# A bias build with both ends of a tile on one engine, and score steps with two pieces instead of four

## The chip, the cores and the metric

The kernel runs on one core of a Trainium2 chip. Its engines are TensorE (PE), which multiplies matrices into the accumulators in PSUM; VectorE (DVE) and ScalarE (ACT), which both read PSUM and SBUF; GpSimd (POOL), which works on SBUF alone; and SyncE (SP), whose queue issues the DMAs here. Each engine takes its instructions in the order in which they were written for it and waits at semaphores for the others. The metric is the device time of one execution, in microseconds (us).

## What is computed

Three layers follow each other: attention with a learned bias by position, and two MLPs that each token passes through. Only attention matters here. There are 4 batches, 8 heads, 576 positions and 64 values a head.

```
scores = scale * np.matmul(q, k.transpose(0, 1, 3, 2))
pos = np.arange(S)
rel = (pos[:, None] - pos[None, :]).astype(np.float32)
psi_rel = np.log1p(np.abs(rel))
psi_i = np.log1p(np.maximum(pos[:, None].astype(np.float32), 1.0))
x = (psi_rel / psi_i)[..., None]
h = np.maximum(x @ w1 + b1, 0.0)
bias = h @ w2
scores = scores + bias.transpose(2, 0, 1)[None, :, :, :]
```

A softmax over the keys and the product with `v` follow. The bias is a sum of 32 hidden relus for every query, distance and head.

## The kernel before

**The bias build** is a generator, `bias_phase`, of 36 steps of 16 queries each (`k` counts them) and one more for the last store. A step is `produce(k)` and `store(k - 1)`. `produce` makes four relu tiles `y`, one for each group of four queries, over N distances, where N falls from 576 to 304 and rises again to 576. The first `na` of the four (one or two) are made by ACT (line 64), the others by DVE (line 66); the list `NA` says how many, and `relu_split` fills it with a greedy plan that adds up estimated costs for both engines. PE then sums the 32 hidden values of each tile (line 71), each group into its own 32 partitions of a PSUM tile `bt`, of which there are two. `store` makes one tile `e` out of `bt`: ACT writes the distances forwards (line 80, 576 - 16k elements), DVE the same distances backwards (line 81, 16k + 15 elements), and SP stores `e` to DRAM (line 83, 295.5 KB). Four tiles `e` go round, and ten relu tiles (`YBUF`). Two small constants `cb`, which the stores add, come out of four matmuls of one column (line 50) that stand behind the first step's sums.

`during(k)` hangs other work into the steps: the loads of the first unit's q, k and v (`load_raw`, `load_v`) and of the identity ahead of the first step, four splits of raw q and k into a high and a low part in steps 6 to 9 (ACT line 170, POOL line 174), two loads of weights in steps 3 and 4, two of the second unit's q and k, and the loads of the finished bias tiles (line 151), which wait for the stores of the rows that they read. 28 steps run alone (`ALONE`), the others four at a time in the first steps of attention: steps 28 to 31 stand ahead of the first scores on PE, 32 to 35 ahead of the second.

**Attention** runs over 16 units, one for each batch and pair of heads. A unit has five steps. In steps 0 to 3 two score tiles are made, for 128 queries of the first head and 128 of the second, each with 64 contraction rows of PE's array so that the two run side by side. The fifth step makes one tile, `t == 8`, for the last 64 queries of both heads, with all 128 rows: q is block diagonal there. q and k are each a high and a low part, so a step has three passes (high-high, low-high, high-low), which add up in PSUM (`scores`, line 213). k is stored with 64 columns at the front for the second head's last keys and 64 at the end for the first head's. So tile 8, which needs both heads' last keys in the same columns, takes them as two pieces of 64 columns, each with zeros in the other head's rows:

```
LAST_TILE = ((0, 64, 288),), ((0, 352, 224), (224, 576, 64), (224, 0, 64))
```

DVE then adds the bias and takes the minimum (`reduce_min`, line 228), ACT takes the exponential, POOL divides by the sum, PE transposes (lines 256 to 265) and multiplies by v (lines 303, 306). Score tiles have two buffers, `sc`, so the scores of a step wait for the reduces of the step before. DVE also carries the conversion of weights for the MLPs in the gaps (lines 493 to 495 and 491).

Of the kernel before, what the change touches and what calls it, by code (L numbers as in the profile page):

```python
# [7 lines left out]
F32 = mybir.dt.float32  # L8
# [19 lines left out]
def bias_phase(tc, pools, par, c_log, bsc, during):  # L28

    nc = tc.nc  # L30
    V, A, G, T = nc.vector, nc.scalar, nc.gpsimd, nc.tensor
    yp, ep, pp, spare = pools
    pr = yp.tile([128, PAR], F32, name="pr", bufs=1)
    nc.sync.dma_start(pr, par)
    lg = yp.tile([128, S], F32, name="lg", bufs=1)
    nc.sync.dma_start(lg, dram_ap(c_log, 0, [[0, 128], [1, S]]))
    during(-1)
    w1c, b1c, wb, ps = pr[:, 0:1], pr[:, 1:2], pr[:, 2:34], pr[:, 34:PAR]
    scl = yp.tile([128, S // 4], F32, name="scl", bufs=1)
    V.tensor_scalar(scl, ps, w1c, None, ALU.mult)  # L40
    nb1 = yp.tile([128, 1], F32, name="nb1", bufs=1)
    V.tensor_scalar(nb1, b1c, -1.0, None, ALU.mult)
    cb = yp.tile([128, 2], F32, name="cb", bufs=1)
    live = {}

    def constants():
        pc = spare.tile([128, 2, 512], F32, name="sc")
        V.memset(cb, 0.0)
        for gr in range(4):
            T.matmul(pc[32 * gr:32 * gr + 32, 0, 0:1], wb, b1c, start=True, stop=True)  # L50
        V.tensor_scalar(cb[64:128, 0:1], pc[64:128, 0, 0:1], 8.0, None, ALU.mult)
        V.tensor_scalar(cb[32:64, 1:2], pc[32:64, 0, 0:1], 8.0, None, ALU.mult)
        V.tensor_scalar(cb[64:128, 1:2], pc[64:128, 0, 0:1], 8.0, None, ALU.mult)

    def produce(k):
        N = max(S - 16 * k, 16 * k + 16)
        na = NA[k]
        bt = pp.tile([128, 2, 512], F32, name="bt")
        ys = []
        for gr in range(4):  # L60
            n = 4 * k + gr
            y = yp.tile([128, S], F32, name="y")
            if gr < na:
                A.activation(y[:, 0:N], lg[:, 0:N], AF.Relu, bias=b1c, scale=scl[:, n:n + 1])
            else:
                V.tensor_scalar(y[:, 0:N], lg[:, 0:N], scl[:, n:n + 1], nb1, ALU.mult, ALU.max)  # L66
            ys.append(y)
        parts = [(0, 0, N)] if N <= 512 else [(0, 0, 512), (1, 512, N - 512)]
        for hf, o, w in parts:
            for gr in range(4):  # L70
                T.matmul(bt[32 * gr:32 * gr + 32, hf, 0:w], wb, ys[gr][:, o:o + w], start=True, stop=True)  # L71
        live[k] = bt, na

    def store(k):
        bt, na = live.pop(k)
        ct = cb[:, 2 - na:3 - na]
        flat = bt.rearrange("p a b -> p (a b)")
        nf, nr = S - 16 * k, 16 * k + 15
        e = ep.tile([128, S + 16], F32, name="e")
        A.activation(e[:, nr:nr + nf], flat[:, 0:nf], AF.Identity, bias=ct, scale=8.0)  # L80
        V.tensor_scalar(e[:, 0:nr], flat[:, nr:0:-1], 8.0, ct, ALU.mult, ALU.add)
        r0 = 128 * (k % 8) * BW
        nc.sync.dma_start(dram_ap(bsc[k // 8], r0 + S - nr, [[BW, 128], [1, nf + nr]]), e[:, 0:nf + nr])

    K = S // 16
    for k in range(K + 1):
        if k < K:
            produce(k)
        if k == 0:
            constants()  # L90
        if k >= 1:
            store(k - 1)
        during(k)
        yield


A0 = 3500.0


def relu_split():  # L100

    a, v = A0, 0.0
    r = []
    for k in range(S // 16):
# [1 line left out]
        n = max(nf, nr + 1)  # L106
        cost = []
        for na in (1, 2):
            cost.append((a + na * (160 + 1.04 * n) + 50 + 1.04 * nf, v + (4 - na) * (180 + 0.54 * n) + 120 + 1.1 * nr, na))
        a, v, na = min(cost, key=lambda x: max(x[:2]))  # L110
        r.append(na)
    return r


NA = relu_split()
PAR = 34 + S // 4
NU = NP * NB
STEP_TILES = ((0, 1), (2, 3), (4, 5), (6, 7), (8,))
# [2 lines left out]
GROUP = (0, 0, 1, 1, 2)  # L121
GW = (256, 320)
QK = S + 64
LAST_TILE = ((0, 64, 288),), ((0, 352, 224), (224, 576, 64), (224, 0, 64))
ON_ACT = (1, 3, 5, 7)


def attention_phase(tc, qT, kT, vP, ident_d, par, c_log, bsc, xs, after_bias, load_weight, filler, tail):
# [5 lines left out]
    with ExitStack() as st, ExitStack() as early:  # L134
# [39 lines left out]
            G.tensor_sub(l, raws.pop((u, i)), h.bitcast(F32))  # L174

        def during(k):
            if k < 0:
                alloc(0)
                for i in range(2):
                    load_raw(0, i)  # L180
# [6 lines left out]
            if k in LW:  # L187
                load_weight()
            for t in range(9):
                if k == min(8 * (t // 2) + 10, S // 16):  # L190
                    load_bias(0, t)

        psr = lambda st, n, k: st.enter_context(tc.tile_pool(name=n, bufs=k, space=PSUM, side="right"))
# [9 lines left out]
        def scores(u, s):  # L203
# [4 lines left out]
            for i, (q, k) in enumerate(((qh, kh), (ql, kh), (qh, kl))):  # L208
                for hf in range(2):
                    for a, t in enumerate(tiles):  # L210
                        r = slice(0, 128) if t == 8 else slice(64 * a, 64 * a + 64)
                        for x, y, n in LAST_TILE[hf] if t == 8 else ((0, 288 * hf + 64 * (1 - a), 288),):
                            T.matmul(sc[u, t][:, hf, x:x + n], q[r, 128 * s:128 * s + 128], k[r, y:y + n],  # L213
                                     start=(i == 0 and x == 0), stop=(i == 2 and x + n == S // 2 and (t < 8 or y < 512)))

        def reduce_min(u, t):
            s = sc.pop((u, t))
# [174 lines left out]
EBUF = 4  # L392
LR = (16, 19)
LW = (3, 4)
YBUF = 10
ALONE = 28
PER = 4
TR = 0
# [429 lines left out]
def _layout(inputs):  # L828
# [10 lines left out]
    qt = np.concatenate([qt[..., :512], tail], axis=3)  # L839
    kw = np.zeros((NB, NP, 128, S + 64), np.float32)  # L840
    kw[:, :, :, 64:576] = kt[..., :512]
    kw[:, :, :64, 576:] = kt[:, :, :64, 512:]
    kw[:, :, 64:, :64] = kt[:, :, 64:, 512:]
    kt = kw
    vp = np.zeros((NB, NP, 128, 5, 2, D), np.float32)
# [33 lines left out]
```

## Time and profile before

| | us |
|---|---|
| time before, median of 3 runs | 1211.99 (1210.79 to 1212.88) |
| profiled execution, its own time | 1211.65 |
| span of the profiled execution | 1209.5 |
| PE busy in the span | 1183.5 |
| DVE busy | 703.9 |
| ACT busy | 623.4 |
| POOL busy | 508.6 |

The span goes from the first to the last instruction of the profiled execution. Busy time of PE counts overlapping matmuls once, up to ends that are modelled; it is no measure of how well PE is used. The bias build fills the first 64 us of the span, the rest of the bias steps and the first score steps the next 20, and attention goes on to about 340 us; the MLPs take the rest. In a row of a timeline or of grouped instructions, what stands in brackets or behind the bar is the idle time of the engine just ahead, and who ended it.

### The profile page before, as it was taken

Reading aid. Unit: us, or ns where it says so; the run is one execution under the profiler, and the core shown is the slowest. Engines: PE = TensorE matmul, PEld = TensorE weight load, DVE = VectorE, ACT = ScalarE, POOL = GpSimd, SP = SyncE. Lnnn points to the kernel's source line nnn. Section 1 sums busy time; section 2 is a strip of 40 time slices with the busy share of each in tenths; the row PEclk is TensorE's granted clock in tenths of the full one; section 3 lists DMA queues with packets and bytes.
Section 4 is the critical chain, followed back from the end, with each engine's and each line's share of the span. In section 5 each row is a group of like instructions: output and inputs, shape, how many; then the busy total and the mean of one; then the engine's idle time right before and its main releaser. Section 6 shows DMA issues by size and latency. Waiting matters only on the chain.

```text
span 1209.5 us, 19450 instructions
## 1 busy us (share of the span) xinstructions
PE 1183.5 (98%) x7280; PEld 1031.9 (85%) x7280; DVE 703.9 (58%) x1237; ACT 623.4 (52%) x1241; POOL 508.6 (42%) x488
## 2 busy tenths in 40 slices
PE   7989999999989999999999999999999999999998
PEld 2257777777769999999999999999999999999997
DVE  6889888888739898898988668872000010010100
ACT  5978778778647766767666556332211111111111
POOL 1037676776535555565555335452211212112111
PEclk9989999999999999999999999999999999999999
DMA  5753636364112323333443322530101001010000
GB/s 164 263 177 116 192 107 207 102 200 121 62 56 79 121 93 122 110 104 122 132 147 109 110 79 91 159 100 17 37 1 40 14 18 36 1 40 14 20 8 27
DMA packets 73261, 112.35 MB, mean 93 GB/s; under 512 B 8528, under 2 KB 51792, under 8 KB 73168
## 3 DMA queue, kind: packets, MB, share of 16 engines
q1 hardware_dynamic: 73168, 111.12, 29.1%
q8 instruction: 58, 0.95, 0.3%
q14 instruction: 35, 0.29, 0.1%
HBM read 81.32 MB, written 29.77 MB: 92 GB/s over the span
## 4 chain that ended last, share of the span: by engine, by line
PE 94%; DVE 2%; ACT 1%; DMA 1%; issue 1%; POOL 0%; SPq 0%; ACTq 0%; POOLq 0%; DVEq 0%
PE up L570 41%; PE acc L647 16%; PE acc L655 12%; PE sc L213 7%; PE pv L306 6%; PE pt L256 6%; PE bt L71 4%; PE pv L303 1%; PE pf L260 1%; DMA lg<-in_c_log 0%; DVE y L66 0%; ACT z L589 0%; PE pf L264 0%; DVE n L228 0%; DMA wraw<-in_wv 0%
## 5 line engine op out<-in xcount | busy, mean ns | idle before, releaser
L570 PE MATMUL up<-xt,w 128*128 128x384 f32 x2880 | 520.5, 335 | 0.5 <-DVE t L615 0.5
L570 PEld LDWEIGHTS up<-xt,w 128*128 128x128 f32 x2880 | 503.8, 188 | 8.0 <-issue 1.2
L625 POOL TENSOR_TENSOR gl<-t,gh 128x384 fp32r<-128x384 f32 x168 | 176.0, 1059 | 470.7 <-ACT gh L624 332.1
L617 DVE TENSOR_TENSOR t<-up,t 128x384 f32<-128x384 f32 x72 | 40.1, 556 | 309.4 <-ACT t L596 309.4
L596 ACT ACTIVATE t<-up 128x384 f32<-128x384 f32 x72 | 35.4, 492 | 332.6 <-PE up L570 332.6
L647 PE MATMUL acc<-gh,w 128*128 128x384 f32 x768 | 195.8, 335 | 2.9 <-ACT z L589 2.9
L246 POOL TENSOR_SCALAR n<-n,rec 128x576 f32<-128x576 f32 x144 | 117.6, 831 | 89.6 <-DVE rec L241 80.0
L647 PEld LDWEIGHTS acc<-gh,w 128*128 128x128 f32 x768 | 138.1, 188 | 4.7 <-ACT z L589 3.8
L655 PE MATMUL acc<-w,gh 128*128 128x512 f32 x432 | 134.3, 392 | 0.0
L647 PE MATMUL acc<-gl,w 128*128 128x384 f32 x384 | 128.4, 334 | 0.0
L228 DVE CUSTOM_DVE_ANT_0 n<-sc,bias 128x576 f32<-128x576 f32 x144 | 103.7, 753 | 41.2 <-PE sc L213 39.1
L235 ACT ACTIVATE n<-n,mn 128x576 f32<-128x576 f32 x144 | 111.5, 784 | 3.5 <-DVE mn L228 3.1
L556 POOL TENSOR_TENSOR xt<-xm,xt 128x384 fp32r<-128x384 f32 x72 | 73.7, 1039 | 62.3 <-ACT xt L555 62.2
L509 POOL TENSOR_TENSOR w<-wu,w 128x512 fp32r<-128x512 f32 x68 | 96.5, 1421 | 7.6 <-ACT w L511 7.6
L655 PEld LDWEIGHTS acc<-w,gh 128*128 128x128 f32 x432 | 80.1, 188 | 13.5
L624 ACT CAST gh<-t 128x384 fp32r<-128x384 f32 x168 | 84.8, 511 | 8.5 <-PE acc L647 3.6
L655 PE MATMUL acc<-w,gl 128*128 128x512 f32 x216 | 85.4, 395 | 0.0
L610 ACT ACTIVATE z<-z,c 128x768 f32<-128x768 f32 x48 | 45.2, 941 | 77.4 <-DVE up L609 77.4
L256 PE MATMUL pt<-ident,n 128*128 128x128 f32 x576 | 81.6, 282 | 1.8 <-DVE at L286 1.8
L611 DVE TENSOR_TENSOR t<-up,t 128x768 f32<-128x768 f32 x48 | 45.9, 957 | 62.8 <-ACT t L589 62.8
L306 PE MATMUL pv<-at,vs 128*64 128x320 f32 (+1 forms) x512 | 80.2, 425 | 0.0
L256 PEld LDWEIGHTS pt<-ident,n 128*128 128x128 f32 x576 | 62.2, 141 | 13.7 <-issue 8.3
(70 smaller groups left out, 1574.6 us busy)
## 6 DMA issues: line engine op xcount, KB each, us to landing
wraw<-in_wo SPq DMA_DIRECT2D x28, 512.0 KB, 3.6
bsc<-e SPq DMA_DIRECT2D x36, 295.5 KB, 2.8
xm<-xs SPq DMA_DIRECT2D x48, 192.0 KB, 3.3
x2s<-o SPq DMA_DIRECT2D x48, 192.0 KB, 3.7
wraw<-in_wi SPq DMA_DIRECT2D x16, 512.0 KB, 4.3
wraw<-in_wg SPq DMA_DIRECT2D x12, 512.0 KB, 3.6
wraw<-in_wv SPq DMA_DIRECT2D x12, 512.0 KB, 3.6
raw<-in_qT SPq DMA_DIRECT2D x16, 320.0 KB, 3.5
```

Source lines behind the costliest of these rows:

```text
L213: T.matmul(sc[u, t][:, hf, x:x + n], q[r, 128 * s:128 * s + 128], k[r, y:y + n], start=(i == 0 and x == 0), stop=(i == 2 and x + n == S // ...
L228: V.tensor_tensor_reduce(n.rearrange("p (a b) -> p a b", a=2), s[:, :, 0:288], bias[t].rearrange("p (a b) -> p a b", a=2), -0.125, 3.0e38, ...
L235: A.activation(n, n, AF.Exp, bias=m, scale=-1.0, accum_out=nsum[u, t // 4][:, t % 4:t % 4 + 1])
L246: G.tensor_scalar(n, n, nrec[u, t // 4][:, t % 4:t % 4 + 1], 1.0, ALU.mult, ALU.mult)
L256: T.transpose(pt[:, i], n[:, o:o + 128], ident)
L306: T.matmul(p[0][64 * a:64 * a + 64, 0:N], v[:, c - 1, a], main[:, c - 1, a * N:a * N + N], start=False, stop=(c == 4))
L509: self.nc.gpsimd.tensor_sub(w[:, 1], u, w[:, 0].bitcast(F32))
L570: T.matmul(p[:, 0:TB], w[:, a, 128 * kt:128 * kt + 128], x[:, c], start=(kt == 0 and i == 0), stop=(kt == 3 and i == 2))
L624: A.copy(h, x[:, j])
L625: G.tensor_sub(l, x[:, j], h.bitcast(F32))
L647: T.matmul(ac[blk][d][:, 0:TB], w[:, a, 128 * d:128 * d + 128], c, start=(begin and j == 0 and i == 0), stop=(end and j == NPR - 1 and i = ...
L655: T.matmul(ac[blk][d], g[:, c], w[:, a], start=(begin and i == 0), stop=(end and i == 2))
```

## The change

- The second head's last keys are stored at the end of k as well as at the front. Tile 8 then has both heads' last keys in its last 64 columns, and each pass has two pieces of 288 columns instead of four.
- `produce` makes the relus alone; the sums have a function of their own, `sums`. A step is now `produce(k)`, `store(k - 2)`, `sums(k)`, and there are 38 of them.
- `store` writes both ends of a tile `e` on one engine, ACT or DVE. The plan, `relu_split`, picks the engine together with the number of relus on ACT, with other estimated costs.
- `constants()` runs ahead of the first step, the first loads of q, k, v and the identity behind step 1, and `YBUF` is 12.

```diff
@@ bias_phase
     nc.sync.dma_start(lg, dram_ap(c_log, 0, [[0, 128], [1, S]]))
-    during(-1)
...
     def produce(k):
         N = max(S - 16 * k, 16 * k + 16)
-        na = NA[k]
-        bt = pp.tile([128, 2, 512], F32, name="bt")
+        na = SPLIT[k][0]
...
+        made[k] = ys
+
+    def sums(k):
+        N = max(S - 16 * k, 16 * k + 16)
+        ys = made.pop(k)
+        bt = pp.tile([128, 2, 512], F32, name="bt")
         parts = [(0, 0, N)] if N <= 512 else [(0, 0, 512), (1, 512, N - 512)]
         for hf, o, w in parts:
             for gr in range(4):
                 T.matmul(bt[32 * gr:32 * gr + 32, hf, 0:w], wb, ys[gr][:, o:o + w], start=True, stop=True)
-        live[k] = bt, na
+        live[k] = bt, SPLIT[k][0]
...
         e = ep.tile([128, S + 16], F32, name="e")
-        A.activation(e[:, nr:nr + nf], flat[:, 0:nf], AF.Identity, bias=ct, scale=8.0)
-        V.tensor_scalar(e[:, 0:nr], flat[:, nr:0:-1], 8.0, ct, ALU.mult, ALU.add)
+        for o, i in ((e[:, nr:nr + nf], flat[:, 0:nf]), (e[:, 0:nr], flat[:, nr:0:-1])):
+            if SPLIT[k][1]:
+                A.activation(o, i, AF.Identity, bias=ct, scale=8.0)
+            else:
+                V.tensor_scalar(o, i, 8.0, ct, ALU.mult, ALU.add)
...
-    for k in range(K + 1):
+    constants()
+    for k in range(K + 2):
         if k < K:
             produce(k)
-        if k == 0:
-            constants()
-        if k >= 1:
-            store(k - 1)
+        if k >= 2:
+            store(k - 2)
+        if k < K:
+            sums(k)
         during(k)
@@ relu_split
-A0 = 3500.0
+A0 = 2000.0
...
-            cost.append((a + na * (160 + 1.04 * n) + 50 + 1.04 * nf, v + (4 - na) * (180 + 0.54 * n) + 120 + 1.1 * nr, na))
+            for out in (0, 1):
+                ca, cv = na * (225 + 1.04 * n), (4 - na) * (225 + 0.54 * n)
+                if out:
+                    ca += 350 + 1.04 * (nf + nr)
+                else:
+                    cv += 280 + 1.05 * (nf + nr)
+                cost.append((a + ca, v + cv, na, out))
@@ during
-            if k < 0:
+            if k == 1:
                 alloc(0)
...
-                if k == min(8 * (t // 2) + 10, S // 16):
+                if k == min(8 * (t // 2) + 10, S // 16 + 1):
                     load_bias(0, t)
@@ scores
-                        for x, y, n in LAST_TILE[hf] if t == 8 else ((0, 288 * hf + 64 * (1 - a), 288),):
-                            T.matmul(sc[u, t][:, hf, x:x + n], q[r, 128 * s:128 * s + 128], k[r, y:y + n],
-                                     start=(i == 0 and x == 0), stop=(i == 2 and x + n == S // 2 and (t < 8 or y < 512)))
+                        o = 288 * hf + (0 if a else 64)
+                        T.matmul(sc[u, t][:, hf, 0:288], q[r, 128 * s:128 * s + 128], k[r, o:o + 288], start=(i == 0), stop=(i == 2))
@@ constants and layout
-YBUF = 10
+YBUF = 12
...
-    kw[:, :, :64, 576:] = kt[:, :, :64, 512:]
+    kw[:, :, :, 576:] = kt[..., 512:]
```

DVE at the start of the build, before (`scl` and `nb_141` are per-query scales and the negative bias of the relus, `cb` the constants):

```order
L40 TENSOR_SCALAR scl<-pr 128x144
L42 TENSOR_SCALAR nb_141<-pr 128x1
L66 TENSOR_SCALAR y<-lg,scl,nb_141 128x576 x3
L48 MEMSET cb 128x2
L51 TENSOR_SCALAR cb<-sc 64x1
L52 TENSOR_SCALAR cb<-sc 32x1
L53 TENSOR_SCALAR cb<-sc 64x1
L66 TENSOR_SCALAR y<-lg,scl,nb_141 128x560 x3
L81 TENSOR_SCALAR e<-bt,cb 128x15
L66 TENSOR_SCALAR y<-lg,scl,nb_141 128x544 x3
L81 TENSOR_SCALAR e<-bt,cb 128x31
```

The same place on DVE after:

```order
L47 MEMSET cb 128x2
L50 TENSOR_SCALAR cb<-sc 64x1
L51 TENSOR_SCALAR cb<-sc 32x1
L52 TENSOR_SCALAR cb<-sc 64x1
L64 TENSOR_SCALAR y<-lg,scl,nb_130 128x576 x3
L64 TENSOR_SCALAR y<-lg,scl,nb_130 128x560 x2
L64 TENSOR_SCALAR y<-lg,scl,nb_130 128x544 x3
L88 TENSOR_SCALAR e<-bt,cb 128x576
L88 TENSOR_SCALAR e<-bt,cb 128x15
L64 TENSOR_SCALAR y<-lg,scl,nb_130 128x528 x3
```

The constants moved ahead of the first relus, and the first tile `e` is whole on DVE, behind the relus of step 2 instead of step 1.

PE in the fifth step of the first unit (`kh`, `kl`, `qh`, `ql` are the high and low parts), before:

```order
L213 MATMUL sc<-kh,qh 128x288
L213 MATMUL sc<-kh,qh 128x224
L213 MATMUL sc<-kh,qh 128x64 x2
L213 MATMUL sc<-kh,ql 128x288
L213 MATMUL sc<-kh,ql 128x224
L213 MATMUL sc<-kh,ql 128x64 x2
L213 MATMUL sc<-kl,qh 128x288
L213 MATMUL sc<-kl,qh 128x224
L213 MATMUL sc<-kl,qh 128x64 x2
L256 MATMUL pt<-ident,n 128x128 x8
```

And after:

```order
L227 MATMUL sc<-kh,qh 128x288 x2
L227 MATMUL sc<-kh,ql 128x288 x2
L227 MATMUL sc<-kl,qh 128x288 x2
L269 MATMUL pt<-ident,n 128x128 x8
L273 MATMUL pf<-ident,n 128x128
```

Twelve matmuls became six; this is so in each of the 16 units, and nothing else moved on PE in attention.

SP's queue at the start, after:

```order
L35 DMA pr<-in_par 128x178
L36 DMA lg<-in_c_log 128x576
L172 DMA raw_180<-in_qT 128x640
L172 DMA raw_182<-in_kT 128x640
L178 DMA vs<-in_vP 128x640
L196 DMA ident<-in_ident 128x128
```

Before, the same six loads stand there in the same order; the move in the program moved nothing in this queue.

## Rows read from the trace of the kernel before

**Rows 1.** The page's head: span and instructions of the profiled execution.

```profile
span 1209.5 us, 19450 instructions
```

**Rows 2.** Busy us (instructions) of PE, PEld, DVE, ACT, POOL; PEclk, DMA share, GB/s.

```profile
6.40:63.50 57.10, 52.96 (x292) 17.08 (x294) 49.66 (x114) 46.97 (x83) 3.10 (x2) 1.00 0.64 223
82.00:84.00 2.00, 2.00 (x11) 2.00 (x11) 1.97 (x2) 0.59 (x2) 2.00 (x3) 0.50 1.01 315
100.00:120.00 20.00, 20.00 (x171) 14.08 (x169) 17.46 (x42) 15.84 (x41) 15.01 (x16) 1.00 0.45 132
```

**Rows 3.** Grouped instructions from 6.4 to 63.5 us: busy, mean ns, idle before.

```profile
L66 DVE TENSOR_SCALAR y<-lg,scl,nb 128x416 f32<-128x416 f32 (+17 forms) x79 | 37.9, 529 | 3.5 <-DMA lg<-in_c_log 3.4
L64 ACT ACTIVATE y<-lg,pr,scl 128x384 f32<-128x384 f32 (+17 forms) x49 | 33.8, 727 | 4.3 <-DMA lg<-in_c_log 4.3
...
L80 ACT ACTIVATE e<-bt,cb 128x576 f32<-128x576 f32 (+30 forms) x31 | 16.6, 537 | 10.0 <-issue 3.1 <-DVE cb L53 2.9 <-ACT y L64 2.1
L81 DVE TENSOR_SCALAR e<-bt,cb 128x15 f32<-128x15 f32 (+30 forms) x31 | 14.9, 481 | 5.0 <-ACT e L80 4.6
```

**Rows 4.** Timeline of the first 12 us, all engines: start, us, what.

```profile
1.17 0.42 SPq L36 DMA_DIRECT2D lg<-in_c_log  x1
...
6.49 1.56 DVE L66 TENSOR_SCALAR y<-lg,scl,nb 128x576 f32<-128x576 f32 x3 [3.43 <-DMA lg<-in_c_log]
...
10.36 0.16 DVE L51 TENSOR_SCALAR cb<-sc 64x1 f32<-64x1 f32 x1 [2.31 <-PE sc L50]
...
10.96 0.74 ACT L80 ACTIVATE e<-bt,cb 128x576 f32<-128x576 f32 x1 [2.85 <-DVE cb L53]
```

**Rows 5.** Timeline of DVE and POOL inside the bias build.

```profile
26.43 2.60 DVE L66 TENSOR_SCALAR y<-lg,scl,nb 128x432 f32<-128x432 f32 x3
...
41.58 0.49 DVE L81 TENSOR_SCALAR e<-bt,cb 128x271 f32<-128x271 f32 x1
41.99 0.78 DVE L66 TENSOR_SCALAR y<-lg,scl,nb 128x304 f32<-128x304 f32 x2
...
26.83 1.55 POOL L174 TENSOR_TENSOR kl<-raw,kh 128x640 fp32r<-128x640 f32 x1 [3.13 <-ACT kh L170]
```

**Rows 6.** DMA issues from 16 to 24 us: KB each, median us to landing.

```profile
bsc<-e SPq DMA_DIRECT2D x4, 295.5 KB, 3.5
wraw<-in_wi SPq DMA_DIRECT2D x2, 512.0 KB, 4.7
```

**Rows 7.** Timeline: DVE's last relus of step 31, PE's first two score steps.

```profile
62.46 0.99 DVE L66 TENSOR_SCALAR y<-lg,scl,nb 128x512 f32<-128x512 f32 x2
...
64.48 0.53 PE L213 MATMUL sc<-kh,qh 64*128 64x288 f32 x4
...
74.14 0.53 PE L213 MATMUL sc<-kh,qh 64*128 64x288 f32 x4
```

**Rows 8.** Chain of work from 140 to 170 us: start, us, what.

```profile
147.31 1.52 PE sc L213 x12
148.83 0.93 PE pt L256 x8
...
151.09 0.99 PE sc L213 x12
152.08 1.02 PE pt L256 x8
...
163.68 1.52 PE sc L213 x12
```

**Rows 9.** Timeline of PE, two passes of a fifth step.

```profile
147.73 0.63 PE L213 MATMUL sc<-kh,ql 128*128 128x288 f32 x4
148.19 0.63 PE L213 MATMUL sc<-kl,qh 128*128 128x288 f32 x4
```

**Rows 10.** Timeline: DVE's reduce of tile 8, PE's next unit.

```profile
149.95 0.74 DVE L228 CUSTOM_DVE_ANT_0 n<-sc,bias 128x576 f32<-128x576 f32 x1
...
151.02 0.53 PE L213 MATMUL sc<-kh,qh 64*128 64x288 f32 x4
```

More of the change, by code (lines that the diff above doesn't have):

```diff
@@ L33, in bias_phase @@
     pr = yp.tile([128, PAR], F32, name="pr", bufs=1)
+    lg = yp.tile([128, S], F32, name="lg", bufs=1)
     nc.sync.dma_start(pr, par)
-    lg = yp.tile([128, S], F32, name="lg", bufs=1)
     nc.sync.dma_start(lg, dram_ap(c_log, 0, [[0, 128], [1, S]]))
-    during(-1)
     w1c, b1c, wb, ps = pr[:, 0:1], pr[:, 1:2], pr[:, 2:34], pr[:, 34:PAR]
@@ L43, in bias_phase @@
     cb = yp.tile([128, 2], F32, name="cb", bufs=1)
-    live = {}
+    live, made = {}, {}
     def constants():
@@ L108, in relu_split @@
         for na in (1, 2):
-            cost.append((a + na * (160 + 1.04 * n) + 50 + 1.04 * nf, v + (4 - na) * (180 + 0.54 * n) + 120 + 1.1 * nr, na))
-        a, v, na = min(cost, key=lambda x: max(x[:2]))
-        r.append(na)
+            for out in (0, 1):
[5 more added lines that the diff above has]
+                cost.append((a + ca, v + cv, na, out))
+        a, v, na, out = min(cost, key=lambda x: max(x[:2]))
+        r.append((na, out))
     return r
-NA = relu_split()
+SPLIT = relu_split()
 PAR = 34 + S // 4
@@ L123 @@
 QK = S + 64
-LAST_TILE = ((0, 64, 288),), ((0, 352, 224), (224, 576, 64), (224, 0, 64))
 ON_ACT = (1, 3, 5, 7)
```

## The prediction

> **What bounds the kernel now.** The page comes first: the profiled execution spans 1209.5 us [rows 1] and was timed at 1211.65 us, 2.15 us more than its span and 0.34 us below the median of the three runs, 1211.99. The sum below is made against 1211.65. The whole change lies in the first 340 us, so the busy times by stretch come next [rows 2]. Between 100 and 120 us PE is busy for 20.00 of 20 us, while DVE has 17.46 and ACT 15.84: attention is bound by PE. In the stretch 6.40 to 63.50, where the position bias is built, nothing is full: DVE is busy 49.66 of 57.10 us, ACT 46.97, and the DMA engines have a share of 0.64. PE's 52.96 there is no bound, since its overlapping pieces count until their modelled ends. Some 7.4 us of DVE's stretch are waits, and the grouped rows name them [rows 3]: 4.6 us before line 81, released by ACT's line 80. Line 81 (DVE) and line 80 (ACT) write the two halves of the same tile `e`, and the row shows DVE held until ACT's half is through. ACT in turn waits 10.0 us before line 80, for sums that PE has only just been given. So the two engines wait for each other once a step. A further 2.31 us on DVE and 2.85 us on ACT go at the start, where both wait for the constants that PE computes only after the first bias sum [rows 4].
>
> **The change, bias build.** Both ends of a tile `e` go to one engine, two steps after its relus. That takes three waits away: DVE on ACT's half, ACT on sums one step old, and, since `constants()` comes first, the wait for the constants. Those need only `pr`; their matmul and the DVE rows behind it fall into the 3.43 us in which DVE waits for `lg` anyway [rows 4], so they cost nothing there.
>
> The work itself hardly changes, only its division. Through step 31, after which the first scores stand, DVE has 79 relus and 30 bias pieces (7410 elements) before, and 84 relus and 24 pieces (7092 elements) after, for 12 tiles. The 79 relus are busy 37.9 us [rows 3]; without two stalls of 1.3 us (below) and without some 0.09 us that the last of each group is held open at its end (30 groups), that is 0.41 each. A bias piece of 271 elements starts at 41.58 and the next instruction at 41.99 [rows 5]: 0.41 us, which I split, as an estimate, into 1 ns an element and 0.14 for the piece. DVE's five more relus are shorter ones, since its columns go from 34.2 to 35.8 thousand (5%): 1.8 us more. It gives up six pieces and 318 elements, 1.1 us: plus 0.7 us in all. Its 49.66 busy us also count the ends of pieces for which the next one waits, those 0.09 us at 30 changes from relu to bias piece, of which 12 are left. I take 49.66 + 0.7 - 2.0 = 48.4 us, within 47.7 (no such end left) and 50.3 (all left).
>
> DVE starts at 6.49 and would then finish step 31 at 54.9 rather than at 63.45 [rows 4, 7]: **8.6 us earlier**, 6.7 to 9.3 by these two bounds. ACT would carry 44 relus, 36 pieces and two casts: it gives up 5 relus (3.7 us at 0.73) and takes 318 elements and 6 pieces (1.1 us), so from its 46.97 it falls to some 44. It is the cover for DVE, with 4 us to spare. One thing there has no row: ACT reading PSUM backwards. Line 80 reads forwards and line 81 backwards, both at some 0.5 us for pieces of some 340 and 250 elements [rows 3], so I price it as forwards; if it cost double, 18 tiles with 4654 such elements by then would add some 4 us, which ACT's 4 us just hold. A gain would change nothing, since ACT is not the late one.
>
> What keeps the freed engines from new waits? PE finishes a step's sums about 1.0 us after the last relu (63.45 against the first score at 64.48 [rows 7]), and a store asks for them two steps, 3.0 us, later. Now PE must wait for a store before it may refill one of two PSUM buffers, where before the store stood a step earlier; behind that wait on PE stand only later sums, which nothing asks for in less than two steps. If this cover were gone, the old pattern would return, up to the 7.4 us of waits. The ring of four `e` tiles asks that a store lands in four steps less the writing, 4 x 1.5 - 1.0 = 5.0 us. Landings were 3.5 us for stores and 4.7 us for weights in the densest stretch [rows 6]. SP's queue meets bias loads one store sooner after the last store that they need, so stores behind them may start some 1.5 us later, four times; the ring holds that. I charge 0.3 us.
>
> Two stalls stay. The three relus at 26.43 take 2.60 us, while POOL's split of 1.55 us runs from 26.83; the same happens once more [rows 5]. POOL's order does not change. This is 1.3 us each, and they are inside the 49.66. The Trainium skill, page "SBUF — State Buffer", section "Who interferes with whom", calls the port pair that DVE and GpSimd share an exclusive lock. By that rule the stall vanishes if a bias piece, read from PSUM, stands there in place of a relu, and the sum would be up to 2.6 us better; this trace shows no such meeting.
>
> The raw q and k, `vs` and `ident` loads are written behind step 1 now, but SP has them in the same place, behind `lg`, with no wait ahead of them. So `lg` lands as late as before (6.49, some 5.3 us after its issue at 1.17 [rows 4]), and I put this edit at nothing. YBUF 12 removes no wait that shows.
>
> From the first score at 64.48 to the second at 74.14 [rows 7], four more bias steps run. There the chain (two reduces, 11 relus and one tile on DVE, the last sums) comes to 9.7 us after, against 9.66 before, and the two tiles left for the third step cost DVE 0.2 us more. I charge 0.2 us.
>
> **The change, attention.** Each of 16 units ends with a step for both heads' last queries. Its three passes have pieces of 288, 224, 64 and 64 columns before, two of 288 after. The chain counts the three passes as 1.52 us, and as 0.99 us in a pair step of 288-column pieces [rows 8]; in the t8 step a pass starts 0.46 us after the one before [rows 9], though 640 columns at full clock (1.00 [rows 2], the 2.4 GHz level) are 0.27 us. So PE's time there does not go by columns: four weight loads a pass do not hide behind pieces of 64. The nearest row is the pair step, which gives 0.53 us less, or 0.44 once its slower handover to the transposes is counted (1.02 instead of 0.93 in the chain). I take 0.48.
>
> The Trainium skill, "TensorE: Matmul & The Clock Gate", section "Back-to-back issue gap", lists about 60 cycles for a matmul of 1 to 64 columns when nothing else binds, 25 ns; by that a pass gets only some 25 ns shorter, and the change is worth 1.2 us in all. The same page's section on LDWEIGHTS (columns over 1.2, 107 ns for 128, so 0.43 us for four) agrees with the 0.46 us of a pass.
>
> How much arrives depends on DVE. The next unit's first scores need the buffer of this step's reduce: in the unit at 147 us the reduce starts at 149.95 and takes 0.74, and PE starts at 151.02, so only 0.33 us is spare [rows 10]. Read so for all units, 0.33 to 0.44 is spare in eight of the thirteen middle ones and 0.5 to 0.9 in five: 8 x 0.39 + 5 x 0.48 = 5.5 us. The first unit runs at half clock (0.50 in its stretch [rows 2]), where PE saves twice as much and 0.8 is spare; in the second, PE is already late by DVE, nothing; the last gives 0.5. **6.8 us**, from 4.5 (DVE's weight work slower beside POOL) to 8.5 (16 x 0.53).
>
> Sum: 8.6 - 0.3 - 0.2 + 6.8 = 14.9 us. 1211.65 - 14.9 = 1196.75, and 0.34 more for the median: **1197.0 us**. The half-clock stretch follows scores that wait, and these stay as sparse; it may grow or go, by about 2 us either way.
>
> **Rivals.** *Columns only*: a score pass costs its columns, so 27 ns are saved in each of 48 passes, 1.3 us: 1202.5. The rows 9 speak against it. *DVE binds attention*: it is busy 87% there [rows 2], and if its order slips at the unit's end only 3 us of 6.8 remain: 1201. *The waits return*: coarse pieces (a tile is 0.9 us on one engine) make PE and both engines wait in turn, and half the bias gain goes: 1201.5; 4 us of spare ACT time speaks against it. *The load order does act*, and `lg` lands 3 us sooner: 1194. *Slower*: the stores bind. If the quicker build pushes 13 MB through the queue so densely that a store lands in L, a step is (L + 1.0)/4. At L = 5.0 it begins to bind; at 6.1 the step is 1.78 us, that of before, and the bias gain is gone; to lose attention's 6.8 us and 2.4 more, 32 steps must each take 0.29 us longer, so from L = 7.3 the kernel is measurably slower. At L = 8 it is 1220 (32 x 2.25 - 57.0 - 6.8 = 8.2 us more). A mean rate of 223 GB/s [rows 2] would become some 263, and the longest landing is 4.7 us.
>
> **How the numbers follow.** Forecast 70%, by itself 1193 to 1200; waits return 11%, DVE binds 6%, columns only 4%, loads act 4%; stores bind, slower, 3%; and 2% that two of these together leave no difference. All but the last two end faster: 95%. The range 1192.5 to 1203 takes in all the faster cases. About 0.2%, 2.4 us, is what a measurement tells from no change.
>
> **What would show it.** The first score near 56 us instead of 64.48; no DVE wait before the bias pieces; the constants ahead of the first relu; `lg` landing at 6.4 as before; passes of about 0.27 us in the t8 step and 15.95 us from one unit's t8 step to the next, where it is 16.37 before (147.31 to 163.68 [rows 8]). Wrong if ACT's backward pieces cost double, if stores land after 5 us, or if PE now waits for DVE's reduce at each unit's start.

## The result, and the profile after

The changed kernel takes **1194.93 us** (median of 4 runs, 1193.72 to 1196.81); the kernel before, on the same chip, 1212.43 (1210.79 to 1214.72). The ratio is 0.9856, 95% interval 0.9835 to 0.9877. The profiled execution took 1194.91 us. Its page begins:

```profile
span 1193.1 us, 19268 instructions
```

So the span is 16.4 us shorter than in [rows 1]. PE's timeline of both kernels says where: the first row of each pair below is of before, the second of after. The pairs are the first unit's tile 8 and the last unit's (start, us, what; in brackets the wait ahead).

```profile
80.98 0.80 PE L213 MATMUL sc<-kh,qh 128*128 128x288 f32 x2 [0.73 <-DVE mn L228]
...
327.46 0.65 PE L213 MATMUL sc<-kh,qh 128*128 128x288 f32 x4
```

```profile
73.01 0.85 PE L227 MATMUL sc<-kh,qh 128*128 128x288 f32 x2 [0.63 <-DVE mn L241]
...
311.19 0.53 PE L227 MATMUL sc<-kh,qh 128*128 128x288 f32 x2
```

Now the start of after: `lg` (the table of log distances that every relu reads), the constants, DVE's last relus of step 31, the first and the second scores.

```profile
1.18 0.42 SPq L36 DMA_DIRECT2D lg<-in_c_log  x1
...
3.20 0.16 DVE L50 TENSOR_SCALAR cb<-sc 64x1 f32<-64x1 f32 x1
...
5.74 3.94 DVE L64 TENSOR_SCALAR y<-lg,scl,nb 128x576 f32<-128x576 f32 x8 [2.04 <-DMA lg<-in_c_log]
...
53.09 0.99 DVE L64 TENSOR_SCALAR y<-lg,scl,nb 128x512 f32<-128x512 f32 x2
53.70 0.90 ACT L86 ACTIVATE e<-bt,cb 128x112 f32<-128x112 f32 x2
54.66 1.07 PE L75 MATMUL bt<-y,pr 128*32 128x512 f32 x8 [0.31 <-ACT e L86]
55.65 0.53 PE L227 MATMUL sc<-kh,qh 64*128 64x288 f32 x4
...
65.44 0.53 PE L227 MATMUL sc<-kh,qh 64*128 64x288 f32 x4
```

With [rows 4] and [rows 7] these rows give the whole account:

| stretch | before, us | after, us | change | predicted |
|---|---|---|---|---|
| `lg` there | 6.49 | 5.74 | -0.75 | 0 |
| `lg` to first scores | 57.99 | 49.91 | -8.08 | -8.3 |
| first to second scores | 9.66 | 9.79 | +0.13 | +0.2 |
| second scores to first tile 8 | 6.84 | 7.57 | +0.73 | 0 |
| first to last tile 8 | 246.48 | 238.18 | -8.30 | -6.3 |
| last tile 8 to the end of the span | 882.04 | 881.91 | -0.13 | -0.5 |
| span | 1209.5 | 1193.1 | -16.4 | -14.9 |

(The predicted attention, 6.8, is parted here into its last unit, 0.5, and the rest.) In the build, the windows and the grouped lines from 6.4 to 54.8 us answer to [rows 2] and [rows 3]:

```profile
6.40:54.80 48.40, 33.15 (x284) 9.73 (x288) 46.24 (x107) 44.10 (x83) 5.07 (x2) 0.96 0.74 261
```

```profile
L64 DVE TENSOR_SCALAR y<-lg,scl,nb 128x496 f32<-128x496 f32 (+17 forms) x83 | 36.7, 509 | 0.0
...
L86 ACT ACTIVATE e<-bt,cb 128x544 f32<-128x544 f32 (+35 forms) x36 | 16.2, 506 | 2.7 <-DMA bsc<-e 1.5 <-PE bt L75 1.1
L88 DVE TENSOR_SCALAR e<-bt,cb 128x576 f32<-128x576 f32 (+23 forms) x24 | 11.4, 514 | 1.4 <-DMA bsc<-e 1.2 <-PE bt L75 0.2
```

DVE's 4.6 us behind ACT's half are gone, and so are its 2.31 and ACT's 2.85 us for the constants. DVE's 1.4 us of waits are nearly all for stores. ACT has about 4.2 us left behind the load of `lg`: 1.5 for stores, 1.1 for sums, and 1.6 ahead of relus. PE, too, now waits for bias tiles inside the build (us in all, times, longest):

```profile
PE bt L75 <- ACT e L86: 8.6, 13, 1.6
PE bt L75 <- DVE e L88: 5.9, 7, 1.2
...
ACT y L62 <- PE bt L75: 1.6, 2, 1.1
```

In attention the chain of waits shows tile 8's step and the next unit's, the answer to [rows 8]:

```profile
168.86 0.99 PE sc L227 x6
169.85 0.87 PE pt L269 x8
...
172.06 0.99 PE sc L227 x12
...
184.64 0.99 PE sc L227 x6
```

Three passes of tile 8 cost 0.99 instead of 1.52 us, the handover 0.87 instead of 0.93, and a unit is 15.78 us instead of 16.37 (147.31 to 163.68).

### The profile page after: what moved, and what is told of

Same layout as the page of the kernel before. It is cut to its first block, busy times and chain, and to the rows that moved or that the text cites. A ratio compares the mean times of both kernels' runs of the same rounds, so it can differ in the third digit from the quotient of the medians.

```text
span 1193.1 us, 19268 instructions
## 1 busy us (share of the span) xinstructions
PE 1153.2 (97%) x7184; PEld 1014.5 (85%) x7184; DVE 698.9 (59%) x1237; ACT 619.2 (52%) x1241; POOL 513.4 (43%) x488
## 4 chain that ended last, share of the span: by engine, by line
PE 91%; DVE 4%; ACT 2%; DMA 1%; issue 1%; POOL 0%; SPq 0%; DVEq 0%; POOLq 0%; ACTq 0%
PE up L583 41%; PE acc L660 16%; PE acc L668 12%; PE sc L227 7%; PE pv L319 6%; PE pt L269 6%; DVE y L64 2%; PE pv L316 1%; PE bt L75 1%; DVE n L241 1%; PE pf L273 1%; DVE e L88 1%; ACT e L86 0%; DMA lg<-in_c_log 0%; ACT z L602 0%
## 5 line engine op out<-in xcount | busy, mean ns | idle before, releaser
L259 POOL TENSOR_SCALAR n<-n,rec 128x576 f32<-128x576 f32 x144 | 120.8, 853 | 79.4 <-DVE rec L254 59.0
```

The lines of the kernel that those rows point to most:

```text
L259: G.tensor_scalar(n, n, nrec[u, t // 4][:, t % 4:t % 4 + 1], 1.0, ALU.mult, ALU.mult)
```

## Experiments

"`lg` to first scores" is below the way from DVE's first relu to PE's first score, each read from that run's timeline: 57.99 us in the trace before, 49.91 after.

### One part of the change alone

**Scores alone.** The kernel before with the new layout of k and two pieces a pass.

```
-for x, y, n in LAST_TILE[hf] if t == 8 else ((0, 288 * hf + 64 * (1 - a), 288),):
-    T.matmul(sc[u, t][:, hf, x:x + n], q[r, ...], k[r, y:y + n], ...)
+o = 288 * hf + (0 if a else 64)
+T.matmul(sc[u, t][:, hf, 0:288], q[r, ...], k[r, o:o + 288], ...)
```

> The kernel before with the score edit alone: keys stored at both ends, two pieces of 288 in each pass of a unit's last step; bias build and load order as before. First score as before, 64.5 us. Theory (from the trace after, where the way from the first unit's t8 step to the last one's fell from 246.5 to 238.2 us): the whole of that belongs to this edit, so the time is 8.3 us below before, some 0.57 us in each of 13 middle units (period 15.78 to 15.80). The prediction's own working: 6.8 us, since DVE's reduce allows only 0.33 to 0.44 in most units (period 15.95); then the 1.5 us between them came with the build edits. Rival columns only: 1.3 us (period 16.29).

Measured: ratio 0.9932 (0.9918 to 0.9946), 8.2 us less (6.5 to 9.9) than the 1211.46 of before on the same chip. The period is again 15.78 us; in its chain of waits one tile 8 and the next are

```profile
144.82 0.99 PE sc L212 x6
145.81 0.87 PE pt L254 x8
...
160.60 0.99 PE sc L212 x6
```

The way from the first to the last tile 8 is 237.94 us, 8.5 less than before. So the gain in attention belongs to this edit alone, the 1.3 us of "columns only" are out, and the prediction's limit by DVE was too tight.

**Build alone.** The kernel after with the four pieces and the old layout.

> The kernel after with the old four-piece t8 step and the old key layout; bias build and load order as after. Theory: first score near 55.7 us as after, t8 period 16.37 as before, time 8 to 9 us below before (DVE's end of step 31 came 9.4 us sooner after, the first t8 step 7.9 us sooner). Rival, the edits help each other: the two single edits together give less than the 17 us of after; then this one gives 6.5 or less.

Measured: 0.9942 (0.9927 to 0.9958), 7.0 us less (5.1 to 8.8). `lg` to first scores is 49.95 us, the period 16.37. The two edits come to 8.2 + 7.0 = 15.2 us against 17.5 (14.9 to 20.0) for both: the intervals overlap, and the traces show no help of one for the other (49.95 and 49.91; 237.94 and 238.18).

**Constants first**, in the kernel before.

```
 K = S // 16
+constants()
 for k in range(K + 1):
...
-        if k == 0:
-            constants()
```

> The kernel before with the constants' matmul and DVE rows moved ahead of the first bias sum, nothing else. Theory: DVE's wait of 2.31 us and ACT's of 2.85 us at the start go and nothing takes their place, first score at 62.1 to 62.3 us (64.48 before), time 2.2 to 2.8 us less. Rival: DVE and ACT still wait for each other once a step, so the head start is eaten by those waits; first score at 63.5 or later, under 1 us less.

Measured: 0.9987 (0.9977 to 0.9997), 1.6 us less (0.4 to 2.8). `lg` to first scores is 56.46, 1.5 us less. Between the theory's 2.2 and the rival's 1: the constants are ready before the first relu, but DVE's next row ahead of line 81 is

```profile
11.13 0.23 DVE L81 TENSOR_SCALAR e<-bt,cb 128x15 f32<-128x15 f32 x1 [1.55 <-ACT e L80]
```

and over the build DVE waits 5.7 us for ACT's halves instead of 4.6. A good third of the head start went into the wait that the rest of the change takes away.

**Loads later**, in the kernel before: the first loads of q, k, v and the identity behind step 1.

```
-    during(-1)
...
-            if k < 0:
+            if k == 1:
                 alloc(0)
```

> The kernel before with the first loads of q, k, vs and ident written behind bias step 1, nothing else. Theory: the queue has them in the same place, so no difference: lg lands at 6.4 to 6.5 us, the first score at 64.5, time within 1 us of before. Rival, the load order acts: lg lands at 5.7 us as in the trace after, first score at 63.7, time 0.75 us less, or up to 3 us less.

Measured: 0.9989 (0.9979 to 1.0), and `lg` there at 4.86 us. It looks like the rival, but all traces together make chance likelier. With the loads written first, `lg` was there at 6.49, 5.92 and 6.58 us (three traces); written later, at 4.37 to 6.56 (eleven traces, the kernel after itself at 5.74 in one and 6.56 in another). SP issues it at 1.17 or 1.18 in all of them. At the same order it spreads by 2.2 us, more than the 1.6 by which it came sooner here than in before; whether the order shifts it by some tenths stays open.

### Which of the build's edits does it

**Both engines write a tile, two steps behind.** The kernel after, but with ACT on the forward half, DVE on the backward half, and the plan of relus of before.

```
-for o, i in ((e[:, nr:nr + nf], flat[:, 0:nf]), (e[:, 0:nr], flat[:, nr:0:-1])):
-    if SPLIT[k][1]:
-        A.activation(o, i, AF.Identity, bias=ct, scale=8.0)
-    else:
-        V.tensor_scalar(o, i, 8.0, ct, ALU.mult, ALU.add)
+A.activation(e[:, nr:nr + nf], flat[:, 0:nf], AF.Identity, bias=ct, scale=8.0)
+V.tensor_scalar(e[:, 0:nr], flat[:, nr:0:-1], 8.0, ct, ALU.mult, ALU.add)
```

> The kernel after, but each bias tile is again divided by its ends as before: ACT takes the forward half, DVE the backward half, with the split of relus of before; the two steps of lag, the constants' place and the scores as after. Theory, sharing the tile makes the wait: DVE is held behind ACT's half once a step although the sums are two steps old, and the 4.6 us before DVE's bias rows come back; first score at 60 to 61 us (55.65 after), time 4 to 6 us above after. Rival, the lag alone made the gain: the sums are there, both halves run at once, and only the pieces are more (30 instead of 24 on DVE and 12 more changes between relu and bias piece, about 1 us): first score at 56.2 to 57.5, time 0.5 to 2 us above after.

Measured: 0.9928 (0.9917 to 0.9939), 8.7 us below before and 8.9 above six tiles with one engine (below) on the same chip. `lg` to first scores is 56.02, 6.1 us more than after: the theory's 4 to 6 us and a little more. The grouped lines up to its first scores show a second cause:

```profile
L84 ACT ACTIVATE e<-bt,cb 128x576 f32<-128x576 f32 (+29 forms) x30 | 16.3, 542 | 8.2 <-DMA bsc<-e 4.6 <-PE bt L75 3.4
...
L85 DVE TENSOR_SCALAR e<-bt,cb 128x15 f32<-128x15 f32 (+29 forms) x30 | 14.2, 472 | 6.9 <-ACT e L84 6.5
```

ACT waits 4.6 us for stores, and DVE, behind ACT's half, waits along.

**The same with six tiles** (`EBUF = 6`) parts the two.

> The kernel in which both engines write each bias tile at two steps of lag, now with a ring of six tiles instead of four. There ACT waited 4.6 us for earlier stores and DVE behind it, 6.5 us, and lg to first score took 56.0 us (49.9 after, 47.9 after with six tiles). Theory, sharing a tile is itself the wait: DVE is held by ACT's half without the ring, lg to first score stays at 52.5 us or more. Rival, sharing only passed the ring's waits on to both engines: without them lg to first score falls to 49 to 50.5 us.

Measured: 0.9885 (0.9867 to 0.9903); `lg` to first scores 52.10.

```profile
L84 ACT ACTIVATE e<-bt,cb 128x576 f32<-128x576 f32 (+29 forms) x30 | 16.5, 549 | 4.6 <-PE bt L75 4.4
...
L85 DVE TENSOR_SCALAR e<-bt,cb 128x15 f32<-128x15 f32 (+29 forms) x30 | 14.1, 470 | 3.0 <-ACT e L84 2.7
```

Without the ring's waits 3.9 us of the loss are gone, and 2.7 us behind ACT's halves stay. Both theories hold a part: sharing a tile is a wait by itself and hands every store's wait to both engines. Against one engine with six tiles (47.84 and 49.53, below) it costs 2.6 to 4.3 us, the older plan of relus included; the plan and the sharing were not tried apart.

**One step behind**, one engine.

```
-        if k >= 2:
-            store(k - 2)
+        if 1 <= k <= K:
+            store(k - 1)
```

> The kernel after with each bias tile written one step behind its sums, not two; still by one engine, everything else as after. Theory, the lag makes the gain: the engine that writes the tile must wait for sums that PE has only just been given, as ACT did before (10.0 us in the stretch), and first score comes at 59 us or later, time 4 us or more above after. Rival, one engine for a tile makes the gain: the relus of the next step lie between and cover the 1.0 us that PE needs, first score at 55.7 to 57, time 0 to 1.5 us above after.

Measured: 0.9881 (0.9867 to 0.9895), 3.0 us above the 0.9856 of six tiles (below) on the same chip. `lg` to first scores is 53.02, 3.1 us more than after and 2.1 more than its repeat below (the first scores at 57.39 owe their place to `lg` at 4.37).

```profile
L86 ACT ACTIVATE e<-bt,cb 128x544 f32<-128x544 f32 (+37 forms) x38 | 17.1, 502 | 6.8 <-PE bt L75 6.2 <-DMA bsc<-e 0.7
L88 DVE TENSOR_SCALAR e<-bt,cb 128x576 f32<-128x576 f32 (+23 forms) x24 | 11.5, 520 | 4.1 <-ACT y L62 1.6 <-PE bt L75 1.5 <-ACT e L86 0.9
```

ACT waits 6.2 us for sums just given, as the theory says, and the time is between theory and rival. So of the 8.1 us (7.1 by the repeat of after) some 1.5 are the constants, 3.4 more come with one engine and its plan at one step of lag, and 2.1 to 3.1 with the second step; the lag without the one engine gives 0.4 (56.46 to 56.02). Two traces of the same kernel differ by 1.0 us here, so none of these is known better than that.

### What still waits

**Six bias tiles** instead of four, in the kernel after (`EBUF = 6`).

> The kernel after with a ring of six bias tiles instead of four. Theory: DVE's wait of 1.2 us and ACT's of 1.5 us for earlier stores go; DVE's comes off the end of step 31, so the first score is at 54.5 us and the time 0.3 to 1.2 us less. Rival: those waits stood where DVE or ACT would next have waited for sums or for the other engine; nothing moves, 0 +- 0.3 us.

Measured: 0.9856 (0.9843 to 0.9869), median 1193.32. `lg` to first scores falls to 47.84, 2.1 us less, and no store's wait is left on DVE or ACT. In time this can't be told from the kernel after.

**Six tiles and another plan**: costs as the traces show them, which moves work from DVE to ACT.

```
-A0 = 2000.0
+A0 = 0.0
-                ca, cv = na * (225 + 1.04 * n), (4 - na) * (225 + 0.54 * n)
+                ca, cv = na * (243 + 0.95 * n), (4 - na) * (190 + 0.52 * n)
-                    ca += 350 + 1.04 * (nf + nr)
+                    ca += 292 + 0.87 * (nf + nr)
-                    cv += 280 + 1.05 * (nf + nr)
+                    cv += 240 + 1.07 * (nf + nr)
```

> The kernel after with a ring of six bias tiles and with the planner's costs set to what the traces show (ACT starts level with DVE, relu 0.95 ns a column on ACT and 0.52 on DVE, bias tile 0.87 and 1.07 ns), which moves work from DVE to ACT, 4 us less busy through step 31. Theory: DVE ends step 31 some 0.7 to 1.3 us sooner than with the six tiles alone, time 1 to 2.5 us below after. Rival: ACT becomes the late engine, its bias tiles come later and PE waits for them; time equal to after or up to 1 us more.

Measured: 0.9856 (0.9843 to 0.9869), the same as six tiles alone. `lg` to first scores 47.80, but the second scores come 11.73 us behind the first, where six tiles alone have 9.81:

```profile
53.88 0.53 PE L227 MATMUL sc<-kh,qh 64*128 64x288 f32 x4
...
58.84 6.84 PE L75 MATMUL bt<-y,pr 128*32 128x512 f32 x64 [3.89 <-DVE e L88]
65.61 0.53 PE L227 MATMUL sc<-kh,qh 64*128 64x288 f32 x4
```

The rival's forecast of the time is right, its mechanism only up to the first scores. DVE ends step 31 some 0.5 us sooner behind `lg` than with six tiles alone, and the first scores gain nothing by it, because PE's last sums wait 0.45 us for ACT's tile. The 1.9 us between first and second scores are not ACT's: it waits 3.2 us for PE's sums there. PE waits 3.89 us for the tile of step 30, which this plan gives to DVE and which stands there behind the reduces of the first scores (57.74 us). The granted clock is also 0.50 from 58 to 64 us in this trace, and no run parts the two.

**Three tiles**, the rival in which stores bind, priced.

> The kernel after with a ring of three bias tiles, to price the rival in which the stores bind. By its sum a step is then (L + 1.0)/3: with landings of 3.3 us 1.43 us, just under the 1.51 us that a step takes after, and 1.6 to 1.7 wherever a bias load holds the queue up. Theory: the ring binds in part, lg to first score 51 to 53 us (49.9 after), time 1 to 3 us above after. Rival, it binds in each step because writing and queueing take longer than 1.0 us: lg to first score over 55 us, time 5 us or more above.

Measured: 0.9915 (0.9897 to 0.9932), 4.5 us above the kernel after on the same chip (0.9878). `lg` to first scores is 53.87, between theory and rival. Up to its first scores:

```profile
L86 ACT ACTIVATE e<-bt,cb 128x544 f32<-128x544 f32 (+35 forms) x36 | 16.2, 503 | 6.8 <-DMA bsc<-e 4.5 <-issue 1.6 <-PE bt L75 0.6
L88 DVE TENSOR_SCALAR e<-bt,cb 128x576 f32<-128x576 f32 (+23 forms) x24 | 11.5, 519 | 5.9 <-DMA bsc<-e 5.0 <-PE bt L75 0.8
```

Even one tile less leaves the kernel 10.3 us faster than before.

**The kernel after again, and six tiles with ten relu buffers**, on one chip.

> The kernel after, once more, beside the next one on the same chip. lg lands anywhere from 4.7 to 6.9 us as in the runs so far if its landing is chance (5.74 in the first trace); lg to first score 49.9 us again, a store wait of 1 to 2.5 us on DVE and on ACT.

> The kernel after with a ring of six bias tiles and ten instead of twelve relu buffers. Theory: YBUF removes nothing, lg to first score 47.9 us as with six tiles and twelve buffers, and the six tiles are worth 1 to 2 us: time 1 to 2 us below the kernel after on the same chip. Rival, the relu buffers bind now that PE waits for bias tiles: lg to first score 49 us or more, time equal to after.

Measured: after 1196.72, 0.9878 (0.9861 to 0.9895); six tiles and ten buffers 1194.65, 0.9865 (0.9846 to 0.9884). Six tiles look 2 us better and the intervals overlap, so that they beat the kernel after is not shown by time, only that `lg` to first scores is shorter in two traces each (50.88 and 49.91 after; 47.84 and 49.53 with six). The repeat missed its expected 49.9 by 1.0 us; DVE's wait for stores is 2.1 us there instead of 1.2. With ten relu buffers DVE meets a wait that no trace with twelve has:

```profile
9.46 1.04 DVE L64 TENSOR_SCALAR y<-lg,scl,nb 128x544 f32<-128x544 f32 x2 [0.66 <-PE bt L75]
```

The rival's 49 us came, then, though only 0.66 of the 1.7 us is this wait; DVE lost another 0.8 us to POOL (below).

## Why the prediction was right, and where its terms were off

The time fell inside the range, 2.1 us below the predicted 1197.0. The build's term was right in size, in part because its errors cancelled: DVE's work came 1.5 us below the forecast, its waits 1.1 above, PE's end 0.5 above. Attention's term was too small, `lg` gave 0.75, as far as the runs tell by chance, and a clock stretch took up to 0.7.

- **DVE's work.** Predicted 48.4 us from `lg` to the end of step 31's relus. Measured 54.08 - 5.74 = 48.34 us, with two things inside that were priced otherwise: waits of 1.4 us (ring 0.3 predicted), and one POOL stall of some 1.6 us where two of 1.3 were to stay.
- **Constants at nothing.** Right: they run at 2.74 to 3.70 us, in the wait for `lg`. The relus and line 88 show no wait for them.
- **"ACT has 4 us to spare."** Its busy time was right (44.10, predicted some 44), the word spare was not. The first scores come 1.57 us after DVE's last relu, not 1.0: PE's sums of step 31 wait for ACT's tile of step 29 (53.70 to 54.60), and the first scores stand behind these sums on PE. The 4.3 us in which ACT is not busy in the stretch are nearly all the waits named above, not spare time. The prediction had put PE's new wait at nothing because only later sums stood behind it; at the end of step 31 the scores do. In the chain of waits from 45 to 60 us ACT's lines 62 and 86 hold 47% of the time, DVE's line 64 10%. That is 0.5 us, and the plan with more work for ACT agrees: there DVE was done sooner and the first scores were not.
- **ACT waits 10.0 us "for sums that PE has only just been given".** The row in [rows 3] names three causes, and PE's sums are not among them. Of the 10.0 us the waits of that stretch put 2.9 down to the constants, which the prediction counts a second time as 2.85, 3.1 to nothing that the profile shows, 2.1 to ACT's own relus, and only 2.0 to sums. No term of the sum rests on it.

```profile
ACT e L80 <- PE bt L71: 2.0, 3, 1.2
```

- **ACT reading PSUM backwards, priced as forwards.** Right: its two pieces take 0.90 us together whether the backward one has 47 or 479 elements.
- **The ring of four: stores within 5.0 us, SP's bias loads 1.5 us late, 0.3 us in all.** The bound was right and was broken: from 33 to 46 us the rows of `e` give

```profile
DMA to landing us min/median/max: 3.2/3.5/6.2
```

  and SP's queue waits at the bias loads for stores to land:

```profile
SPq L165 <- DMA bsc<-e: 3.5, 3, 2.1
```

  The stores behind them start up to 2.1 us late and land late; DVE's tile at 44.58 then waits 1.21 us, for a store issued at 39.77, 1.0 us after its tile was written, that took 4.7 us to land. The term was 0.3 and measured 1.2 on DVE, 2.1 in the repeat; six tiles remove it. The mean rate came as estimated (261 GB/s, predicted 263), the slower rival's landing of 7.3 us did not.

```profile
44.58 0.96 DVE L88 TENSOR_SCALAR e<-bt,cb 128x208 f32<-128x208 f32 x2 [1.21 <-DMA bsc<-e]
```

  The prediction set median landings against the bound; in before, from 6 to 64 us, one store had already taken 5.0:

```profile
DMA to landing us min/median/max: 2.1/2.9/5.0
```

- **"Two stalls stay."** One was left in the trace after. POOL's split of `ql` runs into six relus of DVE, and this time POOL waits: it takes 3.43 us instead of 1.56 and ends soon after DVE's bias tile from PSUM.

```profile
16.86 2.64 DVE L64 TENSOR_SCALAR y<-lg,scl,nb 128x464 f32<-128x464 f32 x6
17.48 3.43 POOL L188 TENSOR_TENSOR ql<-raw,qh 128x640 fp32r<-128x640 f32 x1 [17.04 <-ACT qh L184]
19.42 0.95 DVE L88 TENSOR_SCALAR e<-bt,cb 128x480 f32<-128x480 f32 x2
20.29 2.91 DVE L64 TENSOR_SCALAR y<-lg,scl,nb 128x432 f32<-128x432 f32 x3
20.86 1.68 POOL L188 TENSOR_TENSOR kl<-raw,kh 128x640 fp32r<-128x640 f32 x1
```

  Then the end of `ql`, and `kl`, hold DVE, whose three relus take 2.91 us instead of some 1.3. The rule that the prediction named, the exclusive lock of the Trainium skill's page "SBUF — State Buffer", section "Who interferes with whom", fits in that one engine stands still while the other runs. But the section has the lock held for one instruction, and here POOL, which came during one relu of DVE, waited out four more, until the tile from PSUM began at 19.42. Which engine begins is not settled by the order in the program: with six tiles and ten buffers `ql` and `kl` came through in 1.59 and 1.79 us, and DVE's six relus took 5.10.

- **YBUF removes nothing.** In the trace before no wait for a relu buffer shows. Under the new scheme DVE waits 0.66 us with ten buffers, and ACT's relus wait 1.6 us for PE's sums with twelve as with ten (9.39 and 11.31 us in after). A relu reads nothing that PE writes, so that must be a wait for a free buffer; whether more buffers would shorten the build no run shows.
- **The load order at nothing**: no run decides it, as told above.
- **The step of tile 8, 0.48 (0.44 to 0.53).** It measured 0.59: 0.53 in the passes, and the handover to the transposes fell by 0.06 to 0.87 where the prediction charged 0.09 for a slower one. A pass starts 0.26 to 0.37 us after the one before (184.57, 184.94, 185.20; 0.46 in [rows 9]). In before's pass at 147.24 us the four weight loads start 0.11 to 0.13 us apart, while the second piece of 64 columns starts 0.04 us after the first: what a short piece costs there is its weight load, not its columns nor a fixed price of a piece. The prediction's estimate by the table of the Trainium skill, "TensorE: Matmul & The Clock Gate", section "Back-to-back issue gap", was 1.2 us; the scores alone gave 8.2. The section gives that table for a matmul by itself and says that in a stream weight loads and matmuls set the spacing together, so the measurement speaks against the use of the table here, not against the section.
- **DVE allows only 0.39 in eight middle units, 5.5 us in thirteen.** This is the step that failed: the thirteen gave 7.4 us together, twelve of them all of their 0.57 to 0.60. In [rows 8] and [rows 10] DVE's reduce starts 2.64 us after tile 8's scores (147.31 to 149.95); the prediction took DVE's work ahead of it as fixed. In after it starts 2.07 us after them (184.64 to 186.71), and DVE's weight piece takes 0.68 us, where before it took 1.26. Before:

```profile
147.58 1.91 POOL L246 TENSOR_SCALAR n<-n,rec 128x576 f32<-128x576 f32 x2
147.60 1.26 DVE L495 SCALAR_TENSOR_TENSOR wu<-wraw,wu 128x512 int32<-128x512 int32 x1
```

  And after:

```profile
184.95 0.68 DVE L508 SCALAR_TENSOR_TENSOR wu<-wraw,wu 128x512 int32<-128x512 int32 x1
185.66 1.12 DVE L504 SCALAR_TENSOR_TENSOR wu<-wraw,wu 128x512 int32<-128x512 int32 x1
186.71 0.74 DVE L241 CUSTOM_DVE_ANT_0 n<-sc,bias 128x576 f32<-128x576 f32 x1
```

```profile
184.99 2.40 POOL L259 TENSOR_SCALAR n<-n,rec 128x576 f32<-128x576 f32 x2
```

  In before POOL's two divisions began 0.02 us ahead of DVE's piece and took 1.91 us; now they begin 0.04 us behind it and take 2.40. DVE goes first, POOL pays, and 0.32 us stay spare ahead of the next unit. So it is throughout: of the thirteen middle units POOL begins first in nine before, and in one after, the unit whose tile 8 starts at 279.42 us. There DVE's piece takes 1.15 us, the reduce ends 0.14 us after the next unit's first score, and only 0.39 us are gained, which is what the prediction read for such units. (The first score could start because only the second of the two tiles needs that reduce's buffer; it came 0.2 us behind.) The scores alone show the same (0.83 and 2.33). The second unit came as predicted, beside a DVE that is late, at nothing. The first gave 0.88 us (0.8 predicted), but 1.14 in the repeat of the same kernel, and the half-clock stretch lies differently in it, so the match may be luck. The last unit's 0.5 hardly shows (0.13): its reduce came 0.52 us sooner behind its scores, and where the rest went stays open.

- **The half-clock stretch, about 2 us either way.** Second scores to first tile 8 took 7.57 instead of 6.84 us. The stretch is 6.8 us long in both kernels, but begins 2.4 us ahead of the first tile 8 in after and 0.6 in before, so part of the 0.73 may only have moved here from the first unit. The granted clock is 0.50 there (windows), the 1.2 GHz level, and in after also in a stretch of the build:

```profile
37.00:39.00 2.00, 2.00 (x20) 0.65 (x16) 2.00 (x7) 1.59 (x4) 0.00 (x0) 0.50 0.45 107
72.00:74.00 2.00, 1.37 (x7) 1.03 (x6) 1.81 (x5) 1.01 (x3) 2.00 (x3) 0.50 0.01 4
```

The other rivals: the waits did not return beyond those above, DVE bound attention in one middle unit, for 0.2 us, and a pass did not cost its columns.

## What to carry to other kernels

When two engines write halves of one buffer, one waits for the other (2.7 us here) and for the other's waits; give a tile to one engine and the next tile to the other, and let it come late enough that its input is long done. A short piece costs its weight load (0.11 us here), so lay the data out so that a pass has few pieces. Slack read behind an engine that another can hold up is no firm bound: when some hundredths of a microsecond change which of the two begins first, the other one pays.

## What the runs showed of the hardware that was not expected

- The load of `lg`, issued at 1.17 or 1.18 us in each of 14 traces, was there anywhere from 4.37 to 6.58 us. It moves the whole kernel, and in differences of a microsecond or two it must be taken out by hand.
- The granted clock falls to 0.50 before or in the first unit in every kernel, for some 3 to 10 us, and the more of that lies ahead of the first tile 8, the later it comes: second scores to first tile 8 are 6.84 us in before, 7.57 in after, 7.50 with the constants first and 6.93 with six tiles. In the build it also fell in most kernels with two steps of lag, where PE waits for bias tiles, and in none of those without; that these waits are the cause is not shown, and the build's ends show no loss from it that can be told apart.
- A POOL operation of 1.56 us took 3.43 beside DVE's relus, and DVE's own pieces stretch from 0.68 to 1.26 us by which of the two began some hundredths of a microsecond earlier.
